# Gated linear attention and a rational MLP: v loaded in float32 and rounded on the chip, four buffers of f, and a new order of the steps

## The chip, the cores and the metric

The kernel runs on one NeuronCore of a Trainium2 chip. The core has TensorE (PE, matrix products into PSUM), VectorE (DVE), ScalarE (ACT), GpSimd (POOL) and SyncE (SP, which here only issues transfers). Every engine works through its own queue in order. The metric is the device time of one execution in microseconds; a change in it is called faster or slower from 2% on.

## The reference

The input is four float32 arrays q, k, v and f_logit of shape (4, 8, 768, 48): batch, heads, time, head size. Then the result of the attention, as rows of 384, goes through an MLP with a rational activation.

```python
f = 1.0 / (1.0 + np.exp(-f_logit))
for t in range(S):
    state = f[:, :, t, :, None] * state + np.einsum('bhd,bhe->bhde', k[:, :, t], v[:, :, t])
    y[:, :, t] = np.einsum('bhd,bhde->bhe', q[:, :, t], state)
...
h = x @ w_in                                   # (3072, 384) by (384, 2048)
P = a[0] + a[1] * h + a[2] * h2 + a[3] * h3
Q = 1.0 + np.abs(b[0]) * np.abs(h) + np.abs(b[1]) * h2
g = P / (Q + 1e-06)
return (g @ w_out).astype(np.float32)          # (3072, 2048) by (2048, 384)
```

## The kernel before

The work is cut into 12 units. A unit n is one batch entry (n modulo 4) and 256 steps of time, as two chunks of 128; units of one batch entry follow each other through a carried state. Every unit goes through an attention stage and an MLP stage.

Attention stage: `ld` loads f, k, q (SP's queue, float32) and v. V goes by GpSimd's queue (L220), whose transfer rounds it from float32 to bf16 on the way. `ef` and `ls` (ACT) turn f into log decays; `cs` (PE) sums them over time; `A n 0` and `A n 1` (ACT, L336) give exp of minus and plus these sums, into a ring of two buffers that hold both. `xa n 0` multiplies q, `xa n 1` multiplies k with them (L341; DVE, or POOL where the step says `p`). `T` transposes on PE, `Te` copies the result from PSUM (ACT or DVE). `sc` makes scores, `mk` masks them (DVE), `ic` and `si` make the new state products, `st` scales the state (DVE), `yi` and `yb` make y (PE), with `vm` a small rearranged copy of v. `ye` scales y into x (ACT or DVE).

MLP stage: `h n m0 m1` multiplies x with 128-wide columns m0 to m1 of w_in (L496, four columns are 12 products of 128x256), `hy` copies them out (ACT). `sq` squares (ACT with `s`, else DVE), `ab`, `p1`, `p2`, `pm` build numerator and denominator (DVE). `zv` and `tv` are additions on DVE, `zd` and `ta` the same additions done by transfers that accumulate, issued from POOL. `rc` is the reciprocal (ACT), `gm` the quotient (DVE), `o n j m0 m1` the product with w_out (L590, four columns are 4 products of 128x384 for chunk j), `oe` the eviction and `so` the store. `tl` loads ACT's function tables, `wp` and `wo` load the weights on POOL's queue.

There are four PSUM slots, written `@0` to `@3`; a step that takes a slot waits for the reader of its last content.

What runs when is written out by hand or by a planner in the string `ORDER` (lines 24 to 106): one step after another, and each engine's queue gets its instructions in that order. Loads of SP stand in the same string, so a load whose buffer is still in use holds the loads and stores behind it. `!m5` marks a step and `^m5` makes another, mostly on POOL, begin only when the marked one has ended.

`N_F, N_K, N_Q, N_V = 3, 3, 3, 3` and `N_A = 2` in lines 19 to 21 say how many buffers each ring has.

## Time and profile before

| what | us |
|---|---|
| median of three runs | 216.45 |
| lowest, highest of the three | 214.44, 221.64 |
| the profiled execution's own time | 214.75 |
| its span, from first to last instruction | 213.1 |

All times below come from the one profiled execution, seen from the start of its span. The page of the profile has the busy time of each engine, the span in 40 slices, the transfer queues, the chain of work that ended last and groups of equal instructions; the trace behind it also gives busy time by windows, single instructions in order of time, and who waited for whom. PE is TensorE's products and PEld its weight loads, which overlap. PEclk in the windows is the clock that was granted to TensorE, 1.00 for full. An instruction's duration and its neighbour's overlap a little, so sums of durations are somewhat above busy time.

### The profile page before, as it was taken

To read this page: it belongs to the slowest core of one execution; us is meant where nothing else is said; L and a number is where in the kernel's file an instruction comes from. 1 tells how busy PE (TensorE), PEld (TensorE's weight loads), DVE (VectorE), ACT (ScalarE), POOL (GpSimd) and SP (SyncE) were. 2 spreads that over 40 slices of the span, in tenths; PEclk is the share of its full clock that TensorE was granted. 3 is DMA by queue.
4 is the path that set the end of the run, shared out by engine and by line. 5 is a ranking of instruction groups with operands and counts; after the bars stand their busy time and mean duration, and the time that the engine had idled before them with its cause. 6 is when DMAs were issued, how large, how long until landed. Compare 5 with 4: busy or idle time off the path is not lost.

```text
span 213.1 us, 7168 instructions
## 1 busy us (share of the span) xinstructions
PE 190.6 (89%) x3184; PEld 138.2 (65%) x3184; DVE 185.2 (87%) x215; ACT 185.3 (87%) x196; POOL 80.3 (38%) x86
## 2 busy tenths in 40 slices
PE   0287996997989999999979999999999999999991
PEld 0165675785768857678747765865868767765550
DVE  5149737999979999998999999999999999999960
ACT  3482888998799999999989999999999999979920
POOL 6108600426663082272353513836257331222000
PEclk9999999999799999999999999999999999999999
DMA  5999999999999959999999999999995999899263
GB/s 120 253 235 292 193 201 252 254 261 204 220 207 234 146 115 182 161 258 209 212 215 209 297 168 228 269 213 225 208 221 114 205 207 205 210 213 197 76 148 75
DMA packets 61823, 43.20 MB, mean 203 GB/s; under 512 B 51424, under 2 KB 56544, under 8 KB 61792
## 3 DMA queue, kind: packets, MB, share of 16 engines
q0 software_dynamic: 20528, 23.86, 66.4%
q1 hardware_dynamic: 40976, 18.88, 35.8%
q8 instruction: 25, 0.41, 0.7%
q10 hardware_dynamic: 288, 0.00, 0.1%
q14 instruction: 6, 0.05, 0.1%
HBM read 25.17 MB, written 4.72 MB: 140 GB/s over the span
## 4 chain that ended last, share of the span: by engine, by line
PE 37%; ACT 21%; DVE 20%; DMA 14%; issue 5%; SPq 1%; ACTq 0%; POOL 0%; DVEq 0%; POOLq 0%
PE op L590 16%; PE hp L496 13%; DMA k<-in_k_dram 7%; ACT hy L508 6%; ACT z L534 4%; DMA g<-hy 4%; DVE g L581 3%; ACT A L336 3%; DMA f<-in_f_logit_dram 3%; DVE g L569 3%; ACT L555 2%; DVE h L514 2%; DVE scm L385 2%; PE y L398 2%; DVE g L559 2%
## 5 line engine op out<-in xcount | busy, mean ns | idle before, releaser
L496 PE MATMUL hp<-x,w_in_sb 128*128 128x256 bf16 x576 | 69.8, 277 | 0.2
L590 PE MATMUL op<-w_out_sb,g 128*128 128x384 bf16 x384 | 69.1, 326 | 0.0
L496 PEld LDWEIGHTS <-w_in_sb 128*128 128x128 bf16 x576 | 56.2, 99 | 10.2 <-issue 0.9
L508 ACT CAST hy<-hp 128x1024 bf16<-128x1024 f32 x48 | 47.9, 1030 | 4.6 <-PE hp L496 4.4
L590 PEld LDWEIGHTS <-g 128*128 128x128 bf16 x384 | 35.6, 98 | 22.1 <-DVE g L581 0.4
L534 ACT ACTIVATE z<-z 128x2048 bf16<-128x2048 bf16 x23 | 43.5, 1916 | 1.0 <-DVE z L544 0.9
L573 POOL DMA_DIRECT2D g<-hy x17 | 18.0, 1097 | 38.9 <-issue 13.7
L548 POOL DMA_DIRECT2D z<-h x18 | 20.3, 1256 | 30.6 <-ACT h L513 10.3
L581 DVE TENSOR_TENSOR g<-g,z 128x2048 bf16<-128x2048 bf16 x24 | 29.8, 1248 | 1.7 <-DMA g<-hy 1.0
L385 DVE TENSOR_TENSOR scm<-sc,mask 128x1024 bf16<-128x1024 f32 x24 | 28.7, 1216 | 0.6 <-PE sc L377 0.5
L569 DVE TENSOR_TENSOR g<-g,h 128x4096 bf16<-128x4096 bf16 (+1 forms) x14 | 27.7, 1981 | 0.0
L341 POOL TENSOR_TENSOR qkp<-k,A 128x768 bf16<-128x768 f32 x7 | 12.9, 1845 | 27.9 <-DVE state L487 19.8
L513 ACT ACTIVATE h<-hy 128x2048 bf16<-128x2048 bf16 x11 | 21.1, 1930 | 0.1
L323 PE MATMUL cs<-lsp,Ui 128*128 128x384 bf16 (+1 forms) x39 | 12.1, 373 | 9.4 <-ACT lsp L313 9.4
L336 ACT ACTIVATE A<-cs 128x768 f32<-128x768 f32 (+1 forms) x26 | 19.3, 777 | 0.7 <-PE cs L328 0.7
L559 DVE TENSOR_SCALAR g<-hy,a_sb 128x4096 bf16<-128x4096 bf16 (+1 forms) x14 | 17.3, 1238 | 0.3 <-ACT hy L508 0.3
L355 PE MATMUL tp<-ident,qkp 128*128 128x128 bf16 x192 | 14.6, 234 | 3.2 <-DVE qkp L341 2.6
L564 DVE TENSOR_SCALAR hy<-hy,a_sb 128x4096 bf16<-128x4096 bf16 (+1 forms) x14 | 16.7, 1191 | 0.4
L364 ACT COPY T<-tp 128x1024 f32<-128x1024 f32 (+1 forms) x12 | 11.9, 994 | 4.7 <-PE tp L355 4.5
L514 DVE TENSOR_TENSOR h<-hy 128x2048 bf16<-128x2048 bf16 x13 | 15.8, 1217 | 0.0
L355 PEld LDWEIGHTS <-qkp 128*128 128x128 bf16 x192 | 12.6, 105 | 4.5 <-DVE qkp L341 3.4
L518 DVE TENSOR_SCALAR z<-hy 128x4096 uint16<-128x4096 uint16 (+1 forms) x14 | 15.3, 1094 | 0.1
(74 smaller groups left out, 231.4 us busy)
## 6 DMA issues: line engine op xcount, KB each, us to landing
z<-h POOLq DMA_DIRECT2D x18, 512.0 KB, 8.5
g<-hy POOLq DMA_DIRECT2D x17, 512.0 KB, 7.5
f<-in_f_logit_dram SPq DMA_DIRECT2D x11, 384.0 KB, 6.7
k<-in_k_dram SPq DMA_DIRECT2D x11, 384.0 KB, 8.5
q<-in_q_dram SPq DMA_DIRECT2D x11, 384.0 KB, 6.1
out_dram<-osb SPq DMA_DIRECT2D x22, 192.0 KB, 3.5
v<-in_v_dram POOLq DMA_DIRECT2D x12, 192.0 KB, 9.0
w_in_sb<-in_moe_w_in_dram POOLq DMA_DIRECT2D x8, 192.0 KB, 8.1
```

Of the source, the lines that this page charges most:

```text
L336: nc.scalar.activation(t, src, AF.Exp, scale=1.0 if x else -1.0)
L355: nc.tensor.transpose(t[:, x, i, p, :], s["qk"][:, x, i, 2 * p:2 * p + 2, :].rearrange("t h d -> t (h d)"), ident)
L385: return nc.vector.tensor_mul(t, s["sc", g].rearrange("s r a i t -> s (r a) (i t)"), mb)
L496: nc.tensor.matmul(t[:, m - m0, :].rearrange("f (j t) -> f j t", j=UB), w_in_sb[:, kk, m * P:(m + 1) * P], s["x"][:, :, kk, :], start=(kk ...
L508: nc.scalar.copy(fl(big(s, "hy"), m0, m1), fl(s["hp", m0], 0, m1 - m0))
L513: return nc.scalar.square(fl(big(s, "h2"), m0, m1), fl(big(s, "hy"), m0, m1))
L534: return e.add_instruction(mybir.InstActivation(func=AF.Reciprocal, name=nc.get_next_instruction_name(), engine=mybir.EngineType.Activatio ...
L548: return nc.gpsimd.dma_start(out=fl(big(s, "z"), m0, m1), in_=fl(big(s, "h2"), m0, m1), accum_op=ALU.add)
L559: return nc.vector.tensor_scalar(fl(big(s, "g"), m0, m1), fl(big(s, "hy"), m0, m1), a_sb[:, 3:4], a_sb[:, 2:3], op0=ALU.mult, op1=ALU.add)
L569: return nc.vector.tensor_mul(fl(big(s, "g"), m0, m1), fl(big(s, "g"), m0, m1), fl(big(s, "h2"), m0, m1))
L581: return nc.vector.tensor_mul(fl(big(s, "g"), m0, m1), fl(big(s, "g"), m0, m1), fl(big(s, "z"), m0, m1))
L590: nc.tensor.matmul(s["op", g][:, j, 0:DM], big(s, "g")[:, m, C * j:C * j + C], w_out_sb[:, m, :], start=(s["on", j] == 1), stop=(s["on", j ...
```

## The change

Five things change in the code. V is loaded by SP's queue in float32 into a new ring `vf` of two buffers, and a step `vc` rounds it into `v` (now two buffers): ten times on POOL, once on ACT (unit 9), once on DVE (unit 11). The ring of f has four buffers. Exp of minus the sums (`A n 0`) is written over f of the unit, and the ring of A has three buffers of half the size, for plus the sums only; `xa n 0` reads f's buffer. The string `ORDER` is written anew. Steps `sp` and `du` and a table `s` are defined; the order doesn't use them.

Counted in the two orders, instructions of these steps change engine or number (the numbers for all 12 units):

| step | before | after |
|---|---|---|
| `sq` on ACT, on DVE | 11, 13 | 16 (two of them quarters), 9 |
| `Te` on ACT, on DVE | 12 (one half), 1 half | 10 (two halves), 3 |
| `ye` on ACT, on DVE | 9, 3 | 7, 5 |
| `oe` on ACT, on DVE | 12 (one half), 1 half | 12 (two halves), 1 |
| `xa` on DVE, on POOL | 14, 12 | 16, 10 |
| `vm` on ACT, DVE, POOL | 4, 5, 3 | 3, 7, 2 |
| `vc` on ACT, DVE, POOL | none | 1, 1, 10 |
| `zd`, `ta` | 18, 17 | 20 (two quarters), 16 |
| `zv`, `tv` | 5, 7 | 4, 9 (two quarters) |
| `rc`, `gm`, `ab`, `p1`, `p2`, `pm` | 23, 24, 14 each | 24, 25, 15 each |

The last row's additions are one half of unit 11 cut into two quarters. The numbers of PE's products are the same.

```diff
-N_F, N_K, N_Q, N_V = 3, 3, 3, 3
-N_A, N_T, N_SCM, N_X, N_OSB, N_QK, N_LS = 2, 2, 2, 2, 2, 2, 2
+N_F, N_K, N_Q, N_V, N_VF = 4, 3, 3, 2, 2
+N_A, N_T, N_SCM, N_X, N_OSB, N_QK, N_LS = 3, 2, 2, 2, 2, 2, 2
...
-    rings("A", N_A, [2, 2, DM], F32)
+    rings("vf", N_VF, [H, 2, D], F32)
+    rings("A", N_A, [2, DM], F32)
...
-        eng = {"s": nc.sync, "p": nc.gpsimd, "a": nc.scalar}["p" if what == "v" else qu]
+        eng = {"s": nc.sync, "p": nc.gpsimd, "a": nc.scalar}[qu]
+        what = "vf" if what == "v" else what
...
+    def vc(n, eng="v"):
+        s = unit(n)
+        s["v"] = ring["v"][n % len(ring["v"])]
+        fn = nc.scalar.copy if eng == "s" else (nc.gpsimd if eng == "p" else nc.vector).tensor_copy
+        return fn(s["v"].rearrange("p h i d -> p (h i d)"), s["vf"].rearrange("p h i d -> p (h i d)"))
...
+    def decay(s, x):
+        if x:
+            return s["A1"].rearrange("p i (h d) -> p i h d", h=H)
+        return s["f"].rearrange("p h i d -> p i h d")
...
     def A(n, x, a0=0, a1=HP):
-        s["A", x] = ring["A"][n % len(ring["A"])][:, x]
-        t = s["A", x][:, :, 2 * D * a0:2 * D * a1]
-        src = s["cs", a0][:, :, 0:2 * D * (a1 - a0)]
-        nc.scalar.activation(t, src, AF.Exp, scale=1.0 if x else -1.0)
+        s["A1"] = ring["A"][n % len(ring["A"])]
+        src = s["cs", a0][:, :, 0:2 * D * (a1 - a0)].rearrange("p i (h d) -> p i h d", d=D)
+        nc.scalar.activation(decay(s, x)[:, :, 2 * a0:2 * a1], src, AF.Exp, scale=1.0 if x else -1.0)
```

Of the order, the start as it was, up to the first block of the MLP and the scores of unit 2 (only some of the steps):

```
ab_ b a; ld 0 f 0 2; cz 0; cu 1; ld 0 f 2 4; cz 1; ld 1 f; cz 4; ld 0 v
ld 0 q 0 2; ld 0 q 2 4; cz 5; ci; ld 0 k 2 4; cz 2; cu 0; ld 2 f; ld 0 k 0 2
...
cs 0 2 4 @2; ld 3 f; ae 1; fr; ld 4 f; ld 2 q; A 0 0 2 4; xa 0 1 0 2; ae 0 0 2
...
sc 0 1 @0; ld 5 f; ld 2 k; vm 1; fb; ic 1 @2; st 0 1; xa 1 0 !m3; mk 0 1
T 1 @3; wp 0 8 ^m2; st 1 0; Te 1 s; yb 0; ef 3; yi 1 @3; ye 0 v; ls 3
sc 1 1 @0; wp 8 16 ^m3; ef 5; st 1 1; sc 1 0 @1; ld 2 v; mk 1 1; cs 2 @2; ef 4
ld 3 v; mk 1 0; cs 3 @0; ae 2; cz 3; A 2 1; ls 4; yb 1; A 2 0
h 0 0 4 @1; A 3 0; xa 2 0; ls 5; h 0 4 8 @2; ye 1 v; hy 0 0 4; ld 8 f; ld 3 k
...
h 1 8 12 @3; pm 0 0 8; hy 0 8 12; ae 3; A 3 1; p1 0 8 16; ic 2 @1; sc 2 0 @2; hy 1 8 12
```

And the start as it is now:

```
ab_ b a; ld 0 f 0 2; cu 0; cz 2; ld 0 f 2 4; cz 1; ld 1 f; cz 0; ci; ld 0 k 2 4; ld 0 k 0 2; cu 1; ld 0 q 0 2
ld 1 k; fa; ld 0 q 2 4; ef 0 0 2; cz 4; ld 0 v; ls 0 0 2; ld 2 f; cs 0 0 2 @0; cz 5; ld 1 q; cm; ld 1 v; ld 3 f
ef 1; ld 2 k; ef 0 2 4; ls 0 2 4; A 0 1 0 2; cs 0 2 4 @1; A 0 0 0 2; xa 0 1 0 2; ls 1; xa 0 0 0 2; cz 3
A 0 1 2 4; T 0 0 2 @2; A 0 0 2 4; cs 1 @3; xa 0 1 2 4; Te 0 0 2 s; xa 0 0 2 4 !m0; fr; ld 4 f; ld 2 q
vc 0 p ^m0; A 1 1; T 0 2 4 @2; ld 3 q; ae 0 2 4; ld 3 k; xa 1 1; vm 0 s; ic 0 @1; Te 0 2 4 s; ld 2 v; ae 0 0 2
ab_ a a; sc 0 0 @2; st 0 0 !m1; ae 1; ef 2; yi 0 @0; mk 0 0; wp 0 8 ^m0; A 1 0; st 0 1; ls 2; sc 0 1 @2; mk 0 1
cs 2 @1; wp 8 16 ^m1; xa 1 0 !m2; yb 0; A 2 0; ld 5 f; ae 2; A 2 1; vc 1 p ^m2; ye 0 v; ld 3 v; T 1 @3; fb
ld 4 q; vm 1; ic 1 @1; ld 4 k; Te 1 s; st 1 0; h 0 4 8 @2; sc 1 0 @0; hy 0 4 8; h 0 0 4 @3; mk 1 0; ef 3
yi 1 @2; ls 3; sc 1 1 @0; st 1 1; hy 0 0 4; mk 1 1; cs 3 @1; sq 0 0 8 s; ab 0 0 8; yb 1; p1 0 0 8; h 0 8 12 @3
...
hy 1 0 4; Te 2 v; vc 2 p ^m3; h 1 8 12 @2; ls 4; zd 0 8 16; xa 3 0 !m4; hy 1 12 16; sc 2 0 @3; ld 7 f; mk 2 0
vc 3 p ^m4; hy 1 8 12; T 3 @1; ld 4 v; ic 2 @0; ld 6 f; vm 2; ef 5; ic 3 @3; st 2 0; ld 5 v; p1 0 8 16; yi 2 @2
Te 3 s; ld 5 k; tv 0 0 8; ld 6 k; sq 1 0 8 s; cs 4 @1; ld 6 q; vm 3; st 2 1; pm 0 8 16 !m5; sc 2 1 @0; A 4 0
mk 2 1; ae 4; A 4 1; xa 4 0 0 4 p ^m5; st 3 0 !m6; sc 3 0 @1; yb 2; mk 3 0; xa 4 1 0 4 p ^m6; tl r; rc 0 0 8
yi 3 @0; ye 2 v; sc 3 1 @1; st 3 1; h 2 8 12 @2; wo 4 8; p2 0 8 16 !m7; sq 1 8 16 s; mk 3 1; vc 4 p ^m7
```

In the middle, each product with w_out or w_in keeps its neighbourhood of small products with small shifts. At the end the last steps are, before and now:

```
o 11 0 4 8; o 11 0 8 12; o 11 0 12 16; o 11 1 8 12; oe 11 0 1 v; o 11 1 12 16; so 11 0 1; oe 11 1 2 s; so 11 1 2
...
o 11 1 8 12; gm 11 0 4; o 11 0 8 12 @1; tv 11 4 8; so 10 0 2; o 11 0 12 16; gm 11 4 8; o 11 0 0 4; o 11 0 4 8
o 11 1 4 8; oe 11 0 1 s; o 11 1 0 4; so 11 0 1; oe 11 1 2 s; so 11 1 2
```

158 lines of the change are left out of this document (70 added, 88 removed).

## The prediction

> **What bounds the kernel now.** I read the page's busy shares first, then the windows by stage, then the chain that ended last, and last the groups of instructions for prices.
>
> ```profile
> span 213.1 us, 7168 instructions
> PE 190.6 (89%) x3184; PEld 138.2 (65%) x3184; DVE 185.2 (87%) x215; ACT 185.3 (87%) x196; POOL 80.3 (38%) x86
> PEclk9999999999799999999999999999999999999999
> ...
> 0.00:10.00 10.00, 0.88 (x8) 0.87 (x9) 3.54 (x34) 3.79 (x5) 3.65 (x15) 1.00 0.92 186
> 10.00:40.00 30.00, 25.11 (x493) 18.96 (x493) 20.34 (x31) 22.28 (x35) 8.85 (x12) 1.00 1.16 231
> 40.00:200.00 160.00, 156.22 (x2636) 113.63 (x2635) 155.50 (x146) 155.05 (x153) 67.82 (x60) 0.99 1.07 208
> 200.00:213.10 13.10, 8.44 (x51) 4.69 (x49) 5.86 (x6) 4.21 (x6) 0.00 (x0) 1.00 0.38 91
> ```
>
> Columns of the windows: length, PE, PEld, DVE, ACT and POOL busy, granted clock, DMA share, GB/s. From 40 to 200 us PE, DVE and ACT all work 97% of the time: DVE is idle 4.5 us of 160, ACT 4.95. So an instruction added to DVE or ACT there lengthens the stage by itself, and little idle time is left to win. What is left lies at the ends: from 10 to 40 us DVE idles 30 - 20.34 = 9.7 us and ACT 30 - 22.28 = 7.7 us. POOL, at 38%, bounds nothing.
>
> ```profile
> 17.92 15.14 DMA k<-in_k_dram
> 33.08 0.97 DVE qkp L341
> ...
> 35.16 2.63 PE hp L496 x24
> ...
> 52.60 4.39 PE hp L496 x24
> ...
> 203.10 5.39 PE op L590 x32
> ...
> 208.56 0.48 ACT osb L596
> ```
>
> The chain names two local losses. K of unit 2 is issued at 17.9 us and lands 15 us later, while weights and other loads fill the DMA engines. And 24 products of the first MLP matrix take 4.39 us at 52.6 where the same 24 took 2.63 at 35.2: 1.76 us lost in the stretch where PEclk shows a 7.
>
> **The change, part by part.** Prices of the operations that change engine or number:
>
> ```profile
> L513 ACT ACTIVATE h<-hy 128x2048 bf16<-128x2048 bf16 x11 | 21.1, 1930 | 0.1
> L364 ACT COPY T<-tp 128x1024 f32<-128x1024 f32 (+1 forms) x12 | 11.9, 994 | 4.7 <-PE tp L355 4.5
> L514 DVE TENSOR_TENSOR h<-hy 128x2048 bf16<-128x2048 bf16 x13 | 15.8, 1217 | 0.0
> L341 POOL TENSOR_TENSOR qkp<-k,A 128x768 bf16<-128x768 f32 x7 | 12.9, 1845 | 27.9 <-DVE state L487 19.8 <-DVE hy L564 3.4 <-ACT hy L508 2.1
> L220 POOL DMA_DIRECT2D v<-in_v_dram x12 | 12.9, 1073 | 5.6 <-ACT hy L508 4.0 <-DMA w_in_sb<-in_moe_w_in_dram 1.3 <-issue 0.2
> L313 ACT ACTIVATE lsp<-f 128x768 bf16<-128x768 f32 (+1 forms) x13 | 10.4, 812 | 0.1
> L475 ACT ACTIVATE x<-y 128x768 bf16<-128x768 f32 x9 | 7.3, 814 | 0.0
> L341 DVE TENSOR_TENSOR qkp<-q,A 128x768 bf16<-128x768 f32 (+1 forms) x8 | 6.8, 851 | 6.5 <-ACT A L336 6.3
> L477 DVE TENSOR_SCALAR x<-y,sig 128x768 bf16<-128x768 f32 x3 | 3.0, 1012 | 1.1 <-PE y L398 1.1
> L393 POOL COPY vmp<-v 128x128 bf16<-128x128 bf16 x3 | 0.9, 284 | 5.2 <-DMA v<-in_v_dram 5.2
> L365 DVE COPY T<-tp 128x1024 bf16<-128x1024 bf16 x1 | 0.7, 691 | 1.2 <-PE tp L355 1.2
> ...
> 190.59 3.71 ACT L513 ACTIVATE h<-hy 128x2048 bf16<-128x2048 bf16 x2
> ```
>
> Two squares in a row take 3.71 and not 3.86 us: neighbours overlap by about 0.1 us, which I take off every duration below. Counts are those of the two written orders.
>
> ACT. Squares: 11 halves become 15 (sixteen instructions, two of them quarters): +4 x 1.82 = +7.3. Copies of T: eleven whole and one half become eight and two halves: -3 x 0.92 + 0.5 = -2.3. Scalings of x: nine to seven, -1.4. Evictions of the result lose one whole and gain one half, -0.3. One rounding of v: no row, the nearest is L313 of the same size and types, +0.7 (between 0.2, the small copy of v, and 0.9). One small copy of v less, -0.2; two more splits, +0.2. Sum **+4.0 us**.
>
> DVE. Squares 13 to 9: -4 x 1.12 = -4.5. Three whole copies of T, each estimated at twice L365 less a fixed part, 1.18: +3.5; the half one goes, -0.6. Scalings of x, three to five: +1.8. Products with the decays, two come over from POOL: +2 x 0.85 = +1.7. One half addition to g more, +1.2 with its split; one to z less, -1.1. One whole result eviction for a half, +0.4. One rounding of v, +0.7 (between the 0.1 of a small copy and the 0.9 of L341). Two small copies, +0.2; five splits in unit 11, +0.4. Sum **+3.7 us**.
>
> The two run side by side and both are full, so the longer counts: **+4.0**.
>
> POOL. Twelve issues of v go, -12.9; two products go, -3.7; one small copy, -0.3; two z transfers come and one g transfer goes, about +1. Ten roundings come, each between 0.28 (a sixth of the elements) and 1.85 (the two-input product of the same width); I take 1.2, nearer the middle, so +12. Sum -4, on an engine that is idle 62% of the time: nothing. Its cover is that idle time; without it each late rounding would hold the products with v, and then TensorE.
>
> Loads. SP gets twelve issues of v and the bytes written grow by 12 x 192 KB.
>
> ```profile
> q0 software_dynamic: 20528, 23.86, 66.4%
> ...
> q<-in_q_dram SPq DMA_DIRECT2D x11, 384.0 KB, 6.1
> v<-in_v_dram POOLq DMA_DIRECT2D x12, 192.0 KB, 9.0
> ...
> DVE g L581 <- DMA g<-hy: 1.0, 1, 1.0
> ```
>
> The GpSimd queue alone keeps the DMA engines two thirds busy (SP's loads come on top), and still DVE waits for an accumulated g for 1.0 us in all. A q of the same shape and queue lands in 6.1 us, the v of now in 9.0. So the move could win a little or, at 2.4 MB by the mean 203 GB/s, cost up to 11.6 us of transfer time; nearly all of it is covered by loads issued a unit ahead, and I take zero. Behind which wait SP stands now: ld 4 f waits for the product that reads f of unit 0 (the negative decay is now written over f), ld 7 f for that of unit 3, and v 4, f 6, v 5, k 5, k 6 and q 6 stand behind it. The fourth buffer of f covers this: f 7 is used a stage later. v 4 is the tight one: from the product of unit 3 to its rounding DVE has some 8 us of work, against 6.1 to 9.0 us to land; late by 1 us it would hold POOL and then TensorE's state products of unit 4, DVE and ACT having other work. Decay written over f in runs of 48: L313 writes in such runs at 0.81, so zero (at most 12 x 0.1). Three half-sized buffers of A and two of v instead of three: zero, they are reread a unit later.
>
> The head. K of unit 2 moves ahead of f 4, q 2 and f 5, and w_in ahead of the small work of unit 1. The 2.6 us of DVE idle before 33.08 should go. What is late next is TensorE:
>
> ```profile
> 19.58 1.91 PE L355 MATMUL tp<-ident,qkp 128*128 128x128 bf16 x16 [0.40 <-DVE state L487]
> 24.84 0.53 PE L323 MATMUL cs<-lsp,Us 128*128 128x384 bf16 x1
> ...
> 29.22 2.79 PE L496 MATMUL hp<-x,w_in_sb 128*128 128x256 bf16 x24
> ...
> 46.83 1.07 PE L355 MATMUL tp<-ident,qkp 128*128 128x128 bf16 x16
> 49.21 0.33 PE L323 MATMUL cs<-lsp,Us 128*128 128x384 bf16 x1
> ```
>
> Until 28 us the same small products take almost twice as long as at 47 us, though PEclk prints a 9. The first MLP block, which comes at 29.2 us, is moved up between the small products of unit 1, some 5 us earlier. There it would itself run slowly (24 products 4.4 to 5.3 us), and what stands behind it (scores and y of unit 1) later. So most of the K gain is paid back. Ends: all 7.7 us of ACT's idle time from 10 to 40 goes, or 2.4 us are lost, the small work of unit 1 that now stands behind the first block. I take **-1.0**.
>
> [...] The row: at 52.6 the rate halves after 3.5 us in which TensorE had cs, scores and state products and waits, no block of the MLP. In the new order units 2 and 3 are fused: eleven small blocks from sc 2 0 to sc 3 1 stand together. At warm prices (T 0.9, cs 0.85, yb 0.8, sc 0.37, yi 0.4, ic 0.27) they make about 5.5 us, where now no block after the start is over 2.4. Later blocks are alike in both orders (at most 1.95 against 1.8). So one slow stretch stays, moved: **0**, ends -1.8 (none) and +1.8 (two). [...]
>
> The tail.
>
> ```profile
> 204.29 1.23 DVE L581 TENSOR_TENSOR g<-g,z 128x2048 bf16<-128x2048 bf16 x1
> ```
>
> The last product of DVE is now a quarter: behind it stand 12 products of op (12 x 0.17 = 2.0), 0.5 of eviction, and the 4.1 us from its end to the span's end, 6.5; now, from 204.29 + 1.23 = 205.5 to 213.1, it is 7.6. But the 32 products of the chain run without a gap, TensorE being the last: between -1.1 and 0, **-0.6**.
>
> Sum: 214.75 + 4.0 + 0 - 1.0 + 0 - 0.6 = **217.1 us**. 214.75 is the profiled execution's time (span 213.1 and 1.65 around it); the median of the runs shown is 216.45, 0.8% above it, with 214.44 the lowest. I add nothing for that gap.
>
> **The rivals.** First, the start closes: TensorE's early block warms it sooner, K is there, and ACT's 7.7 us from 10 to 40 go. 214.75 + 4.0 - 7.7 - 0.6 = 210.5. For it speaks the 15 us load; against it the slow prices above. It decides from about 7.7 us saved.
>
> Second, the fused block holds TensorE slow over units 2 to 4, as at the start.
>
> ```profile
> 5.80:28.50 22.70, 16.95 (x350) 12.14 (x350) 12.37 (x24) 14.12 (x26) 9.25 (x13) 1.00 1.17 241
> ...
> 50.00:60.00 10.00, 8.84 (x167) 6.58 (x165) 8.73 (x9) 8.08 (x10) 5.83 (x6) 0.83 1.18 205
> ```
>
> There 17 us of busy PE between 5.8 and 28.5 never raised its rate. The slow stretch of now cost DVE 1.3 and ACT 1.9 us of idle between 50 and 60 (clock 0.83 over the ten); two more such stretches give 217.1 + 3.8 = 221. Slower from 219.0, one stretch more.
>
> Third, POOL's roundings stand in DVE's way.
>
> ```profile
> 16.70 1.80 POOL L341 TENSOR_TENSOR qkp<-k,A 128x768 bf16<-128x768 f32 x1 [5.88 <-DVE state L487]
> 17.69 0.87 DVE L393 COPY vmp<-v 128x128 bf16<-128x128 bf16 x1
> 92.09 0.18 DVE L393 COPY vmp<-v 128x128 bf16<-128x128 bf16 x1
> ```
>
> A DVE copy beside a POOL product took 0.87 instead of 0.18, 0.69 more. Ten times that is 6.9, 224.0; slower than 2% from three of ten. Against it: all ten are marked to begin behind a DVE step, and behind eight of these the next one reads PSUM (a mask product, a copy of T, a scaling of x), like the mask products beside which POOL's products run now. [...]
>
> Fourth, v's new path changes nothing that ends last: that is inside the forecast, at zero.
>
> **How the numbers follow.** A measurement of this kernel tells about 2% from no change, here 210.5 to 219.0. Forecast (close to before) 0.52, first rival 0.17, second 0.21, third 0.10. So faster 0.17, same 0.52, slower 0.31. The range runs from the first rival's time to short of the third's: 210.5 to 222.5.
>
> **What would show it.** ACT busy 189 and DVE 189 us; ACT and DVE still over 96% from 40 to 200 us; K of unit 2 landing by about 25 us; the first MLP block before 27 us and slower than 2.63 per 24; a PEclk digit below 9 near 40 to 50 us; DVE copies of 0.2 not swelling to 0.9. Wrong would be: idle time from 10 to 40 us cut by more than half, or DVE or ACT busy less than before.

## The result, and the profile after

The changed kernel takes 214.16 us (median of 20 runs, 211.48 to 216.26), the kernel before 216.7 (20 runs beside it). The ratio is 0.9882, with a 95% interval of 0.9841 to 0.9922: 1.2% faster, which is less than the 2% that counts as a difference here. Forecast was 217.1, slightly slower; the range held the time, the direction was wrong. Ratios and averages leave disturbed runs out. The kernel before averages 214.2 us in one group of runs below (kernels timed side by side) and 216.1 in another, so a ratio can shift by 0.9% between groups; kernels of one group are compared with each other, kernels of two groups by their profiles too.

The page of the profiled execution (213.26 us, span 211.6), and its windows, with the columns as in the prediction:

```profile
span 211.6 us, 7191 instructions
PE 189.7 (90%) x3184; PEld 137.6 (65%) x3184; DVE 187.3 (89%) x226; ACT 188.5 (89%) x198; POOL 72.3 (34%) x82
PEclk9999999976999999999999999999999999999999
...
0.00:10.00 10.00, 2.52 (x23) 2.26 (x24) 4.68 (x37) 5.89 (x11) 2.18 (x12) 1.00 0.84 222
10.00:40.00 30.00, 26.81 (x529) 21.17 (x527) 22.39 (x31) 22.79 (x33) 8.75 (x13) 1.00 1.08 256
40.00:200.00 160.00, 153.80 (x2609) 110.83 (x2598) 155.36 (x152) 157.00 (x153) 61.37 (x57) 0.98 1.00 215
200.00:211.60 11.60, 6.54 (x39) 3.36 (x36) 4.87 (x7) 2.79 (x5) 0.00 (x0) 1.00 0.41 103
```

Read ACT, the fourth of the busy numbers, stage by stage. Its work grew from 185.3 to 188.5 us, by 3.1. Its idle time fell from 6.2 to 4.1 us in the first ten, from 7.7 to 7.2 up to 40 us, and from 4.95 to 3.0 between 40 and 200; behind 200 it is 8.9 and 8.8. That is 4.6 us of idle time less for 3.1 us of work more, and 1.5 us is the difference of the spans. DVE has 2.1 us more work.

The start, single instructions in order of time (start, duration, in brackets the idle time before and what ended it). First the changed kernel, then the kernel before:

```profile
6.41 1.25 ACT L306 ACTIVATE f<-f 128x768 f32<-128x768 f32 x2 [0.78 <-DMA f<-in_f_logit_dram]
...
12.10 4.63 POOL L226 DMA_DIRECT2D w_in_sb<-in_moe_w_in_dram  x8
...
23.00 1.47 PE L504 MATMUL hp<-x,w_in_sb 128*128 128x256 bf16 x12 [1.84 <-DMA w_in_sb<-in_moe_w_in_dram]
...
24.51 1.01 ACT L521 CAST hy<-hp 128x1024 bf16<-128x1024 f32 x1 [2.82 <-PE hp L504]
```

```profile
8.50 0.84 ACT L308 ACTIVATE f<-f 128x768 f32<-128x768 f32 x1 [2.75 <-DMA f<-in_f_logit_dram]
...
18.45 4.50 POOL L228 DMA_DIRECT2D w_in_sb<-in_moe_w_in_dram  x8
...
30.74 1.01 ACT L508 CAST hy<-hp 128x1024 bf16<-128x1024 f32 x1 [0.76 <-PE hp L496]
```

F of unit 1 is there 2.1 us earlier. The MLP input weights are issued 6.3 us earlier, the first block of the MLP comes at 23.0 instead of 29.2, and ACT's first eviction, behind which ACT has MLP work in its queue, at 24.5 instead of 30.7.

The slow stretch of TensorE's clock did not go. It stands where the forecast put it, at the fused block of units 2 and 3; these are windows of the changed kernel, and one instruction in them:

```profile
40.00:50.00 10.00, 6.72 (x203) 4.72 (x192) 9.22 (x14) 9.97 (x10) 4.74 (x4) 0.74 1.06 257
50.00:60.00 10.00, 9.78 (x186) 8.19 (x184) 9.86 (x10) 9.97 (x13) 4.40 (x5) 0.92 1.18 236
...
48.26 2.72 PE L504 MATMUL hp<-x,w_in_sb 128*128 128x256 bf16 x12 [0.29 <-DVE x L485]
```

The clock was 0.50 from 45 to 52 us, 12 products took 2.72 us, and TensorE was busy only 6.7 us of ten. Yet ACT was idle for 0.03 us in each of the two windows; in the kernel before it had 1.9 us of idle time in the window of its slow stretch (50 to 60).

Groups whose prices had to be guessed (busy time in all, then mean ns of one):

```profile
L219 POOL CAST v<-vf 128x768 bf16<-128x768 f32 x10 | 8.3, 826 | 39.6 <-ACT hy L521 17.9 <-DMA vf<-in_v_dram 8.2 <-ACT vmp L400 7.9
...
L373 DVE COPY T<-tp 128x2048 bf16<-128x2048 bf16 x3 | 3.7, 1219 | 0.0
...
vf<-in_v_dram SPq DMA_DIRECT2D x12, 384.0 KB, 5.1
```

A rounding on POOL takes 0.83 us, not 1.2. A whole copy of T on DVE takes 1.22, where 1.18 was estimated. A v by SP's queue lands in 5.1 us.

### The profile page after: what moved, and what is told of

It is laid out like the page before. It is cut to its first block, busy times and chain, and to the rows that moved or that the text cites. A ratio compares the mean times of both kernels' runs of the same rounds, so it can differ in the third digit from the quotient of the medians.

```text
span 211.6 us, 7191 instructions
## 1 busy us (share of the span) xinstructions
PE 189.7 (90%) x3184; PEld 137.6 (65%) x3184; DVE 187.3 (89%) x226; ACT 188.5 (89%) x198; POOL 72.3 (34%) x82
## 4 chain that ended last, share of the span: by engine, by line
ACT 34%; PE 33%; DVE 15%; DMA 6%; issue 6%; SPq 3%; POOL 1%; DVEq 0%; ACTq 0%; POOLq 0%
PE op L603 14%; PE hp L504 12%; ACT hy L521 9%; ACT z L547 5%; DVE g L594 5%; ACT h L526 5%; DMA w_in_sb<-in_moe_w_in_dram 4%; ACT L568 3%; SPq L212 3%; ACT lsp L311 3%; ACT f L306 3%; DVE g L590 2%; ACT f L344 2%; DMA vf<-in_v_dram 2%; ACT A L344 2%
## 5 line engine op out<-in xcount | busy, mean ns | idle before, releaser
L547 ACT ACTIVATE z<-z 128x2048 bf16<-128x2048 bf16 (+1 forms) x24 | 43.5, 1841 | 0.1
L594 DVE TENSOR_TENSOR g<-g,z 128x2048 bf16<-128x2048 bf16 (+1 forms) x25 | 29.2, 1177 | 0.6
L526 ACT ACTIVATE h<-hy 128x2048 bf16<-128x2048 bf16 (+1 forms) x16 | 28.9, 1818 | 0.2
L582 DVE TENSOR_TENSOR g<-g,h 128x4096 bf16<-128x4096 bf16 (+2 forms) x15 | 27.9, 1859 | 0.1
L586 POOL DMA_DIRECT2D g<-hy x16 | 15.1, 1041 | 24.3 <-DVE hy L577 5.6
L349 POOL TENSOR_TENSOR qkp<-q,f 128x768 bf16<-128x768 f32 x7 | 12.7, 1818 | 24.3 <-DMA out_dram<-osb 8.9
L577 DVE TENSOR_SCALAR hy<-hy,a_sb 128x4096 bf16<-128x4096 bf16 (+2 forms) x15 | 17.1, 1143 | 0.1
L572 DVE TENSOR_SCALAR g<-hy,a_sb 128x4096 bf16<-128x4096 bf16 (+2 forms) x15 | 16.8, 1128 | 0.0
L531 DVE TENSOR_SCALAR z<-hy 128x4096 uint16<-128x4096 uint16 (+2 forms) x15 | 15.1, 1009 | 0.4
L609 ACT COPY osb<-op 128x768 f32<-128x768 f32 (+1 forms) x12 | 9.0, 748 | 5.6 <-PE op L603 5.3
L306 ACT ACTIVATE f<-f 128x768 f32<-128x768 f32 (+1 forms) x13 | 10.5, 814 | 3.3 <-DMA f<-in_f_logit_dram 3.2
```

The lines of the kernel that those rows point to most:

```text
L306: nc.scalar.activation(f, f, AF.Exp, scale=-1.0)
L526: return nc.scalar.square(fl(big(s, "h2"), m0, m1), fl(big(s, "hy"), m0, m1))
L547: return e.add_instruction(mybir.InstActivation(func=AF.Reciprocal, name=nc.get_next_instruction_name(), engine=mybir.EngineType.Activatio ...
L577: return nc.vector.tensor_scalar(fl(big(s, "hy"), m0, m1), fl(big(s, "hy"), m0, m1), a_sb[:, 1:2], a_sb[:, 0:1], op0=ALU.mult, op1=ALU.add)
L582: return nc.vector.tensor_mul(fl(big(s, "g"), m0, m1), fl(big(s, "g"), m0, m1), fl(big(s, "h2"), m0, m1))
L594: return nc.vector.tensor_mul(fl(big(s, "g"), m0, m1), fl(big(s, "g"), m0, m1), fl(big(s, "z"), m0, m1))
```

## The experiments

Every kernel below was timed in five rounds beside the kernel before. "Changed" and "before" in the names say which kernel was edited.

### The parts alone

The changed order with v rounded by its transfer on GpSimd's queue again, as before; the rounding copies are left out:

```diff
-N_F, N_K, N_Q, N_V, N_VF = 4, 3, 3, 2, 2
+N_F, N_K, N_Q, N_V, N_VF = 4, 3, 3, 4, 1
...
-        eng = {"s": nc.sync, "p": nc.gpsimd, "a": nc.scalar}[qu]
-        what = "vf" if what == "v" else what
+        eng = {"s": nc.sync, "p": nc.gpsimd, "a": nc.scalar}["p" if what == "v" else qu]
...
     def vc(n, eng="v"):
+        return []
```

> New order, but v is again rounded by its transfer on GpSimd's queue (ring of four, no rounding copies). Theory S (the start, and slow clock covered by ScalarE's work): the transfer of v 0 stands beside f of unit 1 again, whose first exp comes at 7.5 to 8.5 us instead of 6.4; about half of the gain is lost, ratio to before 0.992 to 0.996. Rival V (the new path of v brings the gain through the whole run, as GpSimd's queue falls from 66 to 54 per cent): all is lost, 0.998 to 1.002. Rival O (the order alone): nothing is lost, 0.986 to 0.990.

Ratio 1.0122 (1.0067 to 1.0178), span 215.4. In its trace:

```profile
3.08 2.86 POOL L211 DMA_DIRECT2D v<-in_v_dram  x3
...
26.10 1.94 PE L504 MATMUL hp<-x,w_in_sb 128*128 128x256 bf16 x12 [1.79 <-DMA w_in_sb<-in_moe_w_in_dram]
```

GpSimd's queue has nothing to wait for at 3.08 us and issues three transfers of v at once, ahead of f and q that are needed first. Between 4.5 and 14 us the transfers moved 220 GB/s (318 in the changed kernel), and the first block comes 3.1 us later than there. The time is outside all three ranges that were expected, beyond that of rival V: the order without the new path lost what it should have won.

The old order with v loaded by SP and rounded on chip:

```diff
-N_F, N_K, N_Q, N_V = 3, 3, 3, 3
+N_F, N_K, N_Q, N_V, N_VF = 3, 3, 3, 2, 2
...
-        eng = {"s": nc.sync, "p": nc.gpsimd, "a": nc.scalar}["p" if what == "v" else qu]
+        eng = {"s": nc.sync, "p": nc.gpsimd, "a": nc.scalar}[qu]
+        what = "vf" if what == "v" else what
...
-sc 0 1 @0; ld 5 f; ld 2 k; vm 1;
+sc 0 1 @0; ld 5 f; ld 2 k; vc 1 p; vm 1;
```

> Old order, but v by SP in float32 and rounded by the same ten copies on GpSimd, one on ScalarE, one on VectorE (two buffers each). Theory S: only the earlier f of unit 1 is won (its exp at 6.5 to 7.5 us), less 0.7 us each for the two copies on ScalarE and VectorE; ratio 0.993 to 1.000. Rival V: 0.986 to 0.990. Rival O: 1.000 to 1.005.

Ratio 1.0103 (1.0035 to 1.0171), above all three ranges, span 213.7. F of unit 1 came at 6.9 us instead of 8.5, but the first block at 29.69, where the old order has it.

```profile
40.00:200.00 160.00, 154.17 (x2620) 112.27 (x2620) 158.18 (x146) 154.02 (x153) 66.97 (x59) 0.99 1.00 216
```

DVE, the third of the busy numbers, has 158.2 us of 160 where it had 155.5, and 189.0 in all where it had 185.2: the new path alone puts work on an engine that was full, and wins nothing back. Its one rounding on DVE is only 0.54 us of the 3.8. Most of the rest is old instructions that take longer: the five small copies of v 0.59 us each on average instead of 0.32 (one took 1.5), the 24 quotients (`gm`) 1.30 instead of 1.25. What stretches them was not tested.

The kernel before with one transfer moved, v of unit 0 behind the first exp of f:

```diff
-ld 1 f; cz 4; ld 0 v
+ld 1 f; cz 4
...
-ef 0 0 2; ld 1 k;
+ef 0 0 2 !m90; ld 0 v ^m90; ld 1 k;
```

> Old kernel with one edit: the transfer of v 0 is issued only after the first exp of f (about 5.2 us instead of 1.7). Theory S: the exp of f of unit 1 starts by 7.2 us instead of 8.5, ScalarE's idle time in the first 10 us falls from 6.2 to about 4.8, ratio 0.992 to 0.996. Rival V and rival O: 1.000; so too if v 0 then comes too late for the first state product (15.4 us).

Ratio 0.9913 (0.9869 to 0.9957), span 213.7. F of unit 1 came at 6.57 us, as in the changed kernel, but the first eviction at 31.1, no earlier than before. The ratio shows a small gain, the averages almost none (214.4 us against 214.8; in this group of runs ratios and averages differ by up to 0.8%), the profiled execution (213.7 against 213.1) none. ACT's idle time fell from 6.2 to 4.4 us in the first ten, and rose from 7.7 to 9.0 between 10 and 40. This execution had no slow stretch at all (the clock was 1.00 from 40 to 200 us), and ACT still idled there for 6.4 us: without a slow stretch the old order is no faster.

### What the first block is worth

The changed kernel with the MLP input weights issued late:

```diff
-yi 0 @0; mk 0 0; wp 0 8 ^m0; A 1 0;
+yi 0 @0; mk 0 0; A 1 0;
...
-cs 2 @1; wp 8 16 ^m1; xa 1 0 !m2;
+cs 2 @1; xa 1 0 !m2; wp 0 8 ^m2; wp 8 16 ^m2;
```

> New kernel with one edit: the eight transfers of w_in begin behind the q product of unit 1 (about 18.3 us, as before the change) instead of behind that of unit 0 (12.1 us). Theory S2 (the gain is the earlier first MLP block: 23.0 us instead of 29.2, at full rate): first block near 29 us, the whole time 4 to 6 us longer, ratio to before 1.007 to 1.018. Rival W (the work that waits is made up later, when the engines are full anyway): 0.988 to 0.993.

Ratio 1.0228 (1.0171 to 1.0285), span 218.7.

```profile
28.68 2.72 PE L504 MATMUL hp<-x,w_in_sb 128*128 128x256 bf16 x12 [4.54 <-DMA w_in_sb<-in_moe_w_in_dram]
...
10.00:40.00 30.00, 20.25 (x402) 15.10 (x401) 14.31 (x22) 15.47 (x25) 6.30 (x10) 0.77 1.03 244
```

The block came 5.7 us later and at half rate, ACT had 7.3 us less done by 40 us, and the span grew by 7.1. In this direction the loss at the start reaches the end whole.

Then the other way, the first half of the weights about 2 us earlier:

```diff
-ls 1; xa 0 0 0 2; cz 3
+ls 1; xa 0 0 0 2 !m30; cz 3
...
-vc 0 p ^m0; A 1 1;
+wp 0 8 ^m30; vc 0 p ^m0; A 1 1;
...
-mk 0 0; wp 0 8 ^m0; A 1 0;
+mk 0 0; A 1 0;
```

> The changed kernel with the first half of the MLP input weights issued about 2.4 us earlier, behind the first full product of unit 0 instead of behind the rounding of v 0 (GpSimd's queue). Theory S2 (each microsecond by which the weights and the first MLP block come earlier is a microsecond of the end, as long as they are what the block waits for): first block near 21.3 us, ratio to the kernel before 0.978 to 0.986. Rival L (the start is bound by the sum of its loads: weights issued earlier push v 0, q, k of unit 2 and f of unit 3 back): first block at 22.5 us or later, or the exp of f of unit 3 later than in the changed kernel by over 1 us, ratio 0.990 or more.

Ratio 1.0148 (1.0056 to 1.024): slower. SP's queue, POOL and TensorE:

```profile
12.86 7.58 SPq L212 DMA_DIRECT2D k<-in_k_dram  x1
...
25.09 0.83 POOL L219 CAST v<-vf 128x768 bf16<-128x768 f32 x1 [7.96 <-DMA vf<-in_v_dram]
...
25.97 0.63 PE L466 MATMUL sv<-v,qkp 64*64 64x48 bf16 x32 [5.61 <-POOL v L219]
26.53 2.74 PE L504 MATMUL hp<-x,w_in_sb 128*128 128x256 bf16 x12
```

(This profiled execution took 220.8 us; the runs behind the ratio took 217.4 to 220.4.) The weights are now issued at 10.07 us, just ahead of v of unit 1 at 10.15, and v is there only at 25 us instead of at 15. POOL's rounding waits for it, the state products behind that rounding wait 5.6 us, and the block stands behind them. So "earlier weights, earlier block" holds only as long as nothing that the block stands behind is pushed back; rival L had it right.

Two kernels leave v alone and move other transfers out of the weights' way. One holds the second half of the weights:

```diff
-cs 2 @1; wp 8 16 ^m1; xa 1 0 !m2;
+cs 2 @1; xa 1 0 !m2;
...
-vc 1 p ^m2; ye 0 v;
+vc 1 p ^m2; wp 8 16 ^m2; ye 0 v;
```

> The changed kernel with the second half of the MLP input weights held behind the rounding of v 1 (issued about 19 us instead of 14.4), so that the first half and the loads of f and K do not share the DMA engines with it. Theory R (the loads of the start stand in one line and the first block waits for what lands last): first block up to 2 us earlier (21.2 to 22.5 us), and the second block, whose weights come later, at 29 us as before or later by under 1 us; ratio 0.980 to 0.990. Rival: the second block then waits for its weights beyond 30 us and pays the gain back, 0.990 to 1.000.

The first block came at 22.59, at half rate (2.72 us for 12), the first eviction at 25.35, and the next block, which needs the second half, at 30.25 (29.09 in the changed kernel). Ratio 1.0024 (0.9975 to 1.0074), the rival's side: nothing is won. The other holds K and q of unit 2 and f of unit 4, with what stands behind them, until the weights are out:

```diff
-ef 1; ld 2 k; ef 0 2 4;
+ef 1; ef 0 2 4;
...
-xa 0 0 2 4 !m0; fr; ld 4 f; ld 2 q
+xa 0 0 2 4 !m0; fr
...
-A 2 0; ld 5 f; ae 2; A 2 1; vc 1 p ^m2;
+A 2 0; ae 2; A 2 1; ld 4 f ^m2; ld 2 k; ld 2 q; ld 5 f; ld 3 q; ld 3 k; ld 2 v; vc 1 p ^m2;
```

> The changed kernel with K of unit 2, f of unit 4 and q of unit 2 (and what stands behind them in SyncE's queue) held until the K product of unit 1 (about 17 us), behind the MLP input weights instead of ahead of and beside them. Theory R: the weights land by about 20.5 us, the first block starts at 21.2 us as soon as the small products before it are done, K of unit 2 is not missed before 30 us, ratio 0.978 to 0.986. Rival K (K of unit 2 early was part of the gain): unit 2's product waits for K, ScalarE idle again between 28 and 36 us, ratio 0.992 or more.

The block came at 21.48, ACT did 24.3 us of work between 10 and 40 us (22.8 in the changed kernel), K of unit 2 was not missed, and the span is 211.0. Ratio 0.9941 (0.988 to 1.0002): the loads behaved as theory R had it, the ratio lies on rival K's side. This is the group in which the kernel before averaged 214.2; the runs of this kernel average 212.8 us beside 214.5 of the kernel above.

### Clock and work

The changed kernel with 30 products that nobody reads, in five places of the fused block of units 2 and 3:

```diff
-T 3 @1; ld 4 v; ic 2 @0;
+T 3 @1; ld 4 v; du 0 6 @0; ic 2 @0;
...
-sc 2 1 @0; A 4 0
+du 0 6 @0; sc 2 1 @0; A 4 0
```

> New kernel with 30 products of 512 columns that nobody reads, six each ahead of five steps of the fused block of units 2 and 3. Theory S: the slow clock stretch at 45 to 51 us goes or shrinks, and the time stays that of the new kernel (ratio to before 0.986 to 0.992), since ScalarE was 99.7 per cent busy there. Rival C (slow clock costs time as it did before, 1.8 us an event): 0.979 to 0.983.

Ratio 1.0043 (1.0002 to 1.0084), span 215.6. Its window, then that of the changed kernel:

```profile
40.00:70.00 30.00, 26.79 (x603) 18.64 (x601) 26.44 (x31) 27.59 (x29) 13.28 (x13) 1.00 1.10 236
```

```profile
40.00:70.00 30.00, 26.03 (x589) 21.07 (x578) 28.98 (x33) 29.94 (x33) 12.81 (x12) 0.89 1.12 238
```

The clock stayed at 1.00 and ACT and DVE got 2.4 and 2.5 us less done: the inserted products stand ahead of the small ones. So this kernel takes the slow stretch away and still doesn't price it: the products cost more than the rate brings.

Four of ACT's squares done twice, 7.3 us of work that nobody needs:

```diff
-sq 5 8 16 s; mk 7 0;
+sq 5 8 16 s; sq 5 8 16 s; mk 7 0;
```

> New kernel with four squares on ScalarE (units 5, 6, 8 and 8) done twice, 4 x 1.8 = 7.2 us of added work on ScalarE between 90 and 160 us. Theory F (a full engine pays one for one, as the prediction's sum had it): ratio to before 1.015 to 1.024. Rival P (TensorE sets the end from 100 us on, and ScalarE's work is partly covered): 0.995 to 1.010.

Ratio 1.0169 (1.0111 to 1.0227), span 216.4. So 7.3 us of work on ACT cost 4.8 us by the spans and 2.9%, some 6 us, by the ratios, which are of two groups. The 3.1 us that the change adds to ACT are a cost, and the order had to win more than that.

Work taken from ACT: two products with the decays to POOL, and two squares to DVE:

```diff
-xa 3 0 !m4; hy 1 12 16;
+xa 3 0 0 4 p !m4; hy 1 12 16;
...
-sq 1 8 16 s; mk 3 1;
+sq 1 8 16; mk 3 1;
```

> New kernel with two products with decays (xa 3 0, xa 5 1) moved from VectorE to GpSimd and two squares of units 1 and 2 moved from ScalarE to VectorE: ScalarE -3.6, VectorE +0.6 us between 35 and 70 us. Theory F: ratio to before 0.972 to 0.982. Rival P, or GpSimd's products of 1.8 us coming late: 0.986 to 0.995.

Ratio 1.0054 (1.001 to 1.0099), span 213.4.

```profile
40.00:70.00 30.00, 26.79 (x607) 21.35 (x604) 29.22 (x31) 26.02 (x29) 17.28 (x14) 0.83 1.02 225
```

ACT lost 2.2 us of work and won 3.9 us of idle time between 40 and 70: the slower product on POOL (2.1 us, at 37.4) comes late for unit 3, and TensorE's transposes wait 1.3 us for it. The slow stretch also became longer, from 41 to 51 us. So less work on ACT was worth nothing here; how much of that is the late product and how much the longer slow stretch, one run doesn't tell.

### The old order with an early block

A start put together by hand on the kernel before (v 0 later, K of unit 2, weights and the first block earlier, the K product of unit 1 on DVE); some of its edits:

```diff
-cs 0 2 4 @2; ld 3 f; ae 1;
+cs 0 2 4 @2; ld 2 k; ld 3 f; ae 1;
...
-T 1 @3; wp 0 8 ^m2; st 1 0;
+yb 0; T 1 @3; wp 0 8 ^m91; wp 8 16 ^m1; ye 0 v; fb; st 1 0;
...
-sc 1 1 @0; wp 8 16 ^m3; ef 5; st 1 1; sc 1 0 @1;
+sc 1 1 @0; ef 5; st 1 1; h 0 0 4 @2; sc 1 0 @1;
```

> Old kernel (v rounded by its transfer, old rings, old work shares) with another start only: v 0 issued after the first exp of f, k 2 ahead of f 3, the k product of unit 1 on VectorE, w_in behind the product of unit 0, y of unit 0 ahead of unit 1's transposes, and the first MLP block ahead of the last scores of unit 1. Theory S2: first MLP block at 23 to 26 us instead of 29.2, ratio to before 0.975 to 0.985, as the old shares need 3 us less of ScalarE. Rival V (the new path of v or the later order brings the gain): 0.993 to 1.003.

Ratio 1.0382 (1.0311 to 1.0452). The block came at 24.5, but the exps of f of units 3 and 5 stand ahead of its eviction in ACT's queue and waited 4.2 and 5.4 us for their loads. So the evictions were put ahead of them, among other shifts; against the kernel above:

```diff
-sc 1 0 @1; ld 2 v; mk 1 1; hy 0 0 4; cs 2 @0; ef 4
+sc 1 0 @1; ld 2 v; mk 1 1; hy 0 0 4; cs 2 @0; ef 3; ls 3
```

> The kernel before with v still rounded by its transfer, but with an early start put together by hand: v 0's transfer issued after the first exp of f, K of unit 2 ahead of f of unit 3, the MLP input weights issued early, the first MLP block early, and on ScalarE the first MLP evictions ahead of the exps and logarithms of f of units 3 to 5, so that late loads of f do not hold them. Theory S2 (the gain is made by the first MLP block coming 6 us earlier, whatever way v takes): first block between 23 and 26 us, ScalarE busy over 21.5 us between 10 and 40, ratio to the kernel before 0.975 to 0.990, better than the changed kernel by up to 1 per cent since ScalarE keeps 3.1 us less work. Rival V (v's new path is needed for the early block to pay): 0.995 or more, with ScalarE idle again before 40 us behind loads.

Ratio 1.0181 (1.0086 to 1.0275).

```profile
24.20 1.01 ACT L364 COPY T<-tp 128x1024 f32<-128x1024 f32 x1 [6.94 <-PE tp L355]
...
29.22 1.01 ACT L508 CAST hy<-hp 128x1024 bf16<-128x1024 f32 x1 [4.01 <-PE hp L496]
```

The rival's side again: ACT waits 6.9 us for the transposes of unit 1, and its first eviction is only 1.5 us earlier than before. An early block by itself is no gain; it has to fit the steps around it. (It also ran at half rate here, 2.74 us for 12 products.) The step that the forecast priced, K of unit 2 alone:

```diff
-cs 0 2 4 @2; ld 3 f; ae 1;
+cs 0 2 4 @2; ld 2 k; ld 3 f; ae 1;
...
-ld 5 f; ld 2 k; vm 1;
+ld 5 f; vm 1;
```

> The kernel before with one transfer moved: K of unit 2 issued ahead of f of unit 3, about 5 us earlier, which was the step that the prediction priced at the start. Rival K (the wait of 2.6 us for K of unit 2 was worth its length): ratio 0.985 to 0.990. Theory S2 (that wait hid nothing that the end depends on, since ScalarE's first MLP eviction does not hang on it): 0.993 to 1.003, with the first MLP block at 29 us as before.

Its six runs took 215.05 to 223.8 us, five of them over 219, too far apart for a ratio. In the profiled execution (220.6 us) an f comes late in place of K:

```profile
31.92 1.57 ACT L308 ACTIVATE f<-f 128x768 f32<-128x768 f32 x2 [7.86 <-DMA f<-in_f_logit_dram]
```

Neither theory is confirmed. The trace says only where K's gain went in that execution: to the load that it overtakes.

### What v's path is for

The new path for v of units 0 to 3 alone; the others are rounded by their transfers, and the float32 buffers of v are laid over those of the result:

```diff
-        eng = {"s": nc.sync, "p": nc.gpsimd, "a": nc.scalar}[qu]
-        what = "vf" if what == "v" else what
+        eng = {"s": nc.sync, "p": nc.gpsimd, "a": nc.scalar}["p" if what == "v" and n > 3 else qu]
+        what = "vf" if what == "v" and n < 4 else what
...
     def vc(n, eng="v"):
         s = unit(n)
+        if n > 3:
+            return []
```

> The changed kernel with the new path of v (loaded unrounded by SyncE's queue, rounded on chip) for units 0 to 3 alone; v of units 4 to 11 is rounded by its transfer again, in GpSimd's queue, and its rounding copies on GpSimd are left out; order as in the changed kernel. Theory S2 (v's path matters only while the first loads stand in line): first block at 23.0 us as in the changed kernel, ratio to the kernel before 0.985 to 0.992. Rival V (the transfers and roundings throughout carry the gain, or the transfers on GpSimd's queue delay other steps later too): 1.00 or more.

The first block came at 22.7 and the ratio is 0.9983 (0.9931 to 1.0035): the start is kept and the gain is not. In the profiled execution (218.2 us, where the runs behind the ratio average 215.2) ACT idles 3.9 us between 100 and 130. The next kernel goes the whole way back to rounding transfers, but holds the first four where SP's queue would have issued them:

```diff
-ef 0 0 2; cz 4; ld 0 v;
+ef 0 0 2 !m40; cz 4; ld 0 v ^m40;
...
-cm; ld 1 v; ld 3 f
+cm; ld 3 f
...
-xa 0 1 0 2; ls 1;
+xa 0 1 0 2 !m41; ld 1 v ^m41; ls 1;
...
-xa 2 1; ae 3; hy 0 12 16
+ld 2 v ^m42; ld 3 v ^m42; xa 2 1; ae 3; hy 0 12 16
```

> The changed kernel with v rounded by its transfer in GpSimd's queue (no rounding copies), as in the first experiment, but with v 0 held until the first exp of f (about 4.6 us), v 1 until the first product of unit 0 (about 9 us), and v 2 and v 3 until the first MLP eviction, so that they are issued about where SyncE issues them in the changed kernel. Theory R (a rounding transfer of v holds the DMA engines longer than a plain one of the same numbers, so that the loads of the start come later wherever it is issued): DMA below 300 GB/s between 4.5 and 14 us (318 in the changed kernel), first MLP block after 24.5 us, ratio to the kernel before 1.00 to 1.01. Rival I (only the early issue of three transfers at 3.1 us hurt in the first experiment): about 318 GB/s, first block at 22 to 23.5 us, ratio 0.985 to 0.993.

Ratio 1.0017 (0.9961 to 1.0074), span 214.4. The rate between 4.5 and 14 us was 281 GB/s, below 300 as theory R had it; but the first block came at 22.45, as rival I had it. Only the early issue had hurt the start, and the lower rate was enough. And yet the ratio is theory R's. Its trace, then its window of 120 to 135 us:

```profile
126.63 0.97 PE L504 MATMUL hp<-x,w_in_sb 128*128 128x256 bf16 x6 [2.34 <-issue]
...
127.64 1.01 ACT L521 CAST hy<-hp 128x1024 bf16<-128x1024 f32 x1 [3.15 <-PE hp L504]
...
120.00:135.00 15.00, 12.66 (x231) 9.61 (x228) 11.40 (x11) 10.77 (x11) 4.52 (x4) 0.89 1.14 217
```

TensorE stands still for 2.34 us between the sixth and the seventh product of an MLP block of unit 7, waiting for nothing that the profile names, and the next products are slow. ACT idles 4.2 us of the 15. The kernel of the experiment before had the same wait of 2.34 at the same product. Just ahead of it, at 109 and 118 us, GpSimd's queue issues the rounding transfers of v 10 and v 11. So only these two were moved:

```diff
-zd 4 8 16; ld 10 v; ld 10 k;
+zd 4 8 16; ld 10 k;
...
-zd 5 0 8; ld 11 v; o 3 1 4 8;
+zd 5 0 8; o 3 1 4 8;
...
-hy 7 8 12; T 9 @2; so 3 0 2;
+hy 7 8 12 !m50; T 9 @2; ld 10 v ^m50; ld 11 v ^m50; so 3 0 2;
```

> The kernel of the held rounding loads (changed order, v rounded by its transfer) with only the transfers of v 10 and v 11 moved behind one MLP eviction of unit 7 (about 127 us instead of 109 and 118). That kernel had the early first block of the changed kernel and yet lost its gain between 124 and 134 us, where TensorE stood 2.34 us in the middle of the MLP block of unit 7 with nothing that the profile names as the cause, and then ran slowly. Theory G (the gain is given back there because the rounding transfers hold the DMA engines that something of TensorE's waits for): the wait in that block falls to 1.3 us or less, ScalarE's idle time between 120 and 135 us to below 2.5 us, and the ratio to the kernel before to 0.985 to 0.993. Rival N (the wait has nothing to do with these two transfers): wait of 2 us or more, ratio 0.997 or more.

Ratio 0.9828 (0.9776 to 0.9879), span 211.5.

```profile
126.13 1.01 ACT L521 CAST hy<-hp 128x1024 bf16<-128x1024 f32 x1 [0.41 <-PE hp L504]
...
120.00:135.00 15.00, 14.96 (x280) 10.71 (x278) 15.00 (x15) 14.18 (x13) 7.07 (x7) 1.00 1.20 220
```

The wait is gone, ACT idles 0.8 us there instead of 4.2, the span is 2.9 us shorter, and the average falls from 214.6 to 212.5, in another group. Moving the two transfers took the loss away, as theory G had it; its mechanism is not shown by that. Other kernels with the changed order have or lack the same wait without a change to these transfers:

```profile
131.58 1.18 PE L504 MATMUL hp<-x,w_in_sb 128*128 128x256 bf16 x6 [2.24 <-issue]
...
129.35 0.83 PE L504 MATMUL hp<-x,w_in_sb 128*128 128x256 bf16 x6 [0.95 <-issue]
...
125.22 1.48 PE L504 MATMUL hp<-x,w_in_sb 128*128 128x256 bf16 x12
```

The first is the kernel with early weights: 2.24 us, and its v never goes by GpSimd's queue. The second is the first experiment: 0.95 us, with v 10 and v 11 rounded by transfers at the same steps as in the held kernel. The third is the kernel with squares done twice: no wait at all.

The end of this wait goes with one kind of transfer in the traces. Each trace has 25 packets of 16 KB in queue 8, which the page calls "instruction". In the changed kernel one of them begins at 123.46 us, and the seventh product starts at 125.72, 2.26 us later, behind a wait of 1.19. In the eleven profiled executions with this wait, the seventh product starts 2.2 to 2.4 us behind the beginning of one such packet. In the three without it (squares twice, the inserted products, v 10 and v 11 moved) that packet began earlier, 3.0 to 4.3 us ahead of the product. And all 28 waits of TensorE over 0.3 us for which the 20 profiled executions name no cause end 2.2 to 2.5 us behind the beginning of such a packet (in the kernel before at 28.87 and 51.26 us, with packets at 26.68 and 48.83). What the packets carry is not shown; that TensorE waits for it is the author's inference from these times. The three executions with a wait of 2.2 to 2.3 us in that block are also the only ones with a clock of 0.50 right behind it, for 3.4 us.

With its transfers in these places the old way of v does as well as the new one: the changed kernel itself, timed beside it, had

> The changed kernel as it is, on the chip of the two others of this call, as the measure for them: ratio to the kernel before 0.984 to 0.993 as when the change was timed; first MLP block at 22 to 23 us.

ratio 0.9896 (0.9834 to 0.9959), the first block at 22.27, and 2.1 us of ACT's idle time between 120 and 135. The third kernel of that group is the one with K, q and f held, again:

> The kernel that holds K and q of unit 2 and f of unit 4 behind the MLP input weights, beside the changed kernel on one chip. If the 1.5 us by which its first MLP block came earlier is worth its length, it is faster than the changed kernel by 0.3 to 0.7 per cent; if that start only meets a later wait (TensorE's in the MLP block of unit 7 near 125 us was 1.81 us there and 1.19 us in the changed kernel), the two agree within 0.3 per cent.

Ratio 0.9804 (0.9739 to 0.9869), span 210.7.

```profile
21.58 1.47 PE L504 MATMUL hp<-x,w_in_sb 128*128 128x256 bf16 x12 [0.83 <-DMA w_in_sb<-in_moe_w_in_dram]
...
124.89 0.83 PE L504 MATMUL hp<-x,w_in_sb 128*128 128x256 bf16 x6 [1.82 <-issue]
```

Its five runs average 211.9 us against 213.6 of the changed kernel's five, 0.8%, a little over what was expected; the intervals of the two ratios overlap, and the wait near 125 us takes part of the gain back. It is the fastest kernel here beside the one with v 10 and v 11 moved. The two edits together were not tried.

## Why the prediction was wrong

The sum was 214.75 + 4.0 + 0 - 1.0 + 0 - 0.6. Term by term, against ACT's accounts in the two profiles:

| term | forecast | measured | how |
|---|---|---|---|
| work added (ACT) | +4.0 | +3.1 | busy 185.3 to 188.5 |
| head | -1.0 | -2.6 | idle time before 40 us, 13.9 to 11.3 |
| the middle, put at 0 for the clock | 0 | -1.95 | idle time 40 to 200 us, 4.95 to 3.0 |
| tail | -0.6 | -0.1 | idle time behind 200 us |

**The steps that failed are the head, at "I take -1.0", and the middle, put at 0 with the clock.** The head brought 1.6 us more than was taken, the middle 1.95 us more. Neither alone turns the direction: with only the head as measured the sum is 215.5 us, with only the middle 215.2, both above 214.75; with the two it is 213.6.

**The head** was given one gain, K of unit 2, and most of it was taken back because the moved-up block "would itself run slowly (24 products 4.4 to 5.3 us)". Both halves were wrong. The block ran at full rate in the profile of the changed kernel (1.47 and 1.48 us per 12). The trace's first record of TensorE's clock, at 1.00, begins there at 21.0 us, ahead of the block; in the kernel before it begins at 28.7. Where the block ran slowly (1.99 and 2.31 in the kernel with v 10 and v 11 moved), the time was no worse. And K was not what mattered: holding K of unit 2 behind the weights in the changed order made the kernel faster, if anything. What the forecast gave no gain were two other moves: v 0's transfer lay ahead of f of unit 1, which came 2.1 us earlier without it, and the weights came 6.3 us earlier. Of the 2.6 us, 2.1 lie ahead of 10 us, where f comes. The kernel before with v 0 alone moved won nearly as much there (1.8 us) and gave 1.3 back before 40 us, where its first block had not moved. The late weights show what their place is worth, 7.1 us of span for a first block 5.7 us later and at half rate.

**The middle and the clock.** The place was right, one stretch at 45 to 52 us, but it was twice as long: 6.8 us at 0.50 against 3.4 before. The price was wrong the other way: it was held at what it costs in the kernel before (1.9 us of ACT's idle time), while ACT was busy through it, its first MLP work having come six microseconds sooner. That ACT's queue covers it is read from the two windows; no run took the cover away without something else changing.

**The work.** +3.1 on ACT and +2.1 on DVE instead of +4.0 and +3.7. That it must be paid was right, at 4.8 to 6 us for 7.3 by the doubled squares. The lone new path in the old order put work on DVE in the same way.

**Loads, at "I take zero".** This zero hid what a load's place is worth. In the changed order neither way of v is dear by itself; its place is. Three early transfers cost the start 3.1 us (the first experiment), and the held kernel took 2.9 us more span than the one with v 10 and v 11 moved, nearly all of it near 125 us. SP's queue gives v a place in one line with f, K and q, and so avoids the first. The wait near 125 us is there with it too: 1.2 and 1.5 us in the changed kernel, 2.24 with early weights.

**Roundings and the tail.** 0.83 us each on POOL and no small copy of DVE swollen (0.18 to 0.25 us for the seven of v): the third rival did not show. It may have in the old order, where the same roundings left small copies of 0.59 us on average. The tail's -0.6 came as -0.1 in ACT's account. By the forecast's own measure, from the end of DVE's last product to the end of the span, the bound at -1.1 came: 6.5 us instead of 7.6. The reason given for 0 did not hold: the chain there goes through DVE, 12 products of TensorE, which waits 0.4 us for DVE's last, and the eviction.

**Rivals and signs.** The first, the start closes, asked for 7.7 us between 10 and 40 us; 0.5 came there and 2.1 ahead of it. Its reason was half right: TensorE's clock stood at 1.00 sooner (first record at 21.0 us against 28.7), but ahead of the early block, which began at 23.0. The second's slow stretches did not multiply, though the one was longer. K of unit 2 landed at 28.0 us and not by 25; its product began at 32.7 and did not wait for it. Neither of the signs that were named for being wrong came: ACT and DVE were busier than before (188.5 and 187.3 us), and the idle time from 10 to 40 us was cut by far less than half (7.7 to 7.2 for ACT). ACT's gain came ahead of 10 us and behind 40, where the forecast did not look.

**Still open** is what makes the 16 KB packet ahead of the seventh product in that block of unit 7 late. It was late with the two rounding transfers ahead of it and early with them moved, but as late in a kernel that has no such transfers. So how moving them took the wait away is not shown.

## What to carry to other kernels

Price a moved load by what it stands ahead of, not by the operation that waits for it now: the same bytes of v cost the start 3.1 us in one place and nothing in another. Where one engine is full, as ACT is here (157.0 us of 160), look for what starts it: a first block 5.7 us later and at half rate cost 7.1 us of span. And price a slow stretch elsewhere by the idle time that it brings there: 1.9 us in the kernel before, 0.06 in the changed one. Test "both parts are needed" by giving the old part the new part's timing, before crediting the part.
